# Loading the attention inputs and up-weights first, and moving a weight product behind the first feed-forward tiles

## The chip, the cores and the metric

The kernel runs on one core of a Trainium2 chip. The metric is the device time of one execution in microseconds. The profile adds the span of the core (about 2 us shorter than the time) and the start and duration of every instruction. PE is the matmul engine (TensorE), DVE is VectorE, ACT is ScalarE, POOL is GpSimd, SP is the engine that issues the loads.

## The reference, cut to what matters

```python
# attention: a retention recurrence per batch and head, 4 x 8 x 768 x 64
state = gamma * state + k_t (outer) v_t
y_t   = scale * q_t @ state
# feed-forward on x = y as 3072 x 512
h   = (x @ w1) * (x @ w2) @ w3      # w1, w2: 512 x 1024, w3: 1024 x 1024
out = h @ w_out                      # w_out: 1024 x 512
```

`w3` and `w_out` act one after the other with nothing in between, so the kernel multiplies them once (`W3O = w3 @ w_out`, 64 matmuls of 512 columns and 64 transposes) and uses `W3O` afterwards. The question is *when* that product is made.

## The kernel before

The sequence is cut into 24 chunks of 128 tokens. A chunk needs casts of q, k and v, transposes of q and k, `scores`, the state update `kv`, and `outputs`, which yields x. The feed-forward works on tiles of tokens (0 to 256, 256 to 384, 384 to 512, then 256 each): `a_unit` (w1), `b_unit` (w2, multiplied with the a-half on DVE into `HT`), `o_unit` (`HT` with `W3O`, written out).

```python
# loads, all issued by SP in this order
for i in range(4):
    w3c_st.append(load_w3_columns(i)); wo_st.append(load_wo(i))
w3_st = {f: load_rows(moe_w3, f) for f in range(4, 8)}
load_pair(0)                                   # q, k, v of chunks 0 and 1
w1_st = [load_rows(moe_w1, d) for d in range(4)]
load_pair(1, "qk")
w2_st = [load_rows(moe_w2, 0)]
load_pair(1, "v")
w2_st += [load_rows(moe_w2, d) for d in range(1, 4)]
for n in range(4, 8): load_chunk(n)
# ... constants, cut ...
cast_w3(("c", 0), w3c_st[0])
busy(8)                                        # 8 dummy products on zeros
w3_transpose_columns(0); cast_wo(0)
# ... cut ...
busy(5)
w3_mm_columns(0, acc, lambda: w3_transpose_columns(1))
# ... the rest of the w3 product; from w3_mm(6) on, chunks 0 and 1 are woven in ...
w3_mm(7, chunk1_scores)
# ... tile 0 by weight rows (by_rows), as w1 and w2 land, woven with chunks 2 and 3; cut ...
for i in range(4):
    nc.vector.tensor_tensor(f0.HT[:, 2*i:2*i+2, :], pa[i], ps[i], MULT)
outputs(3, "psA1"); f1.a_unit(6, "psA0"); casts(4)
Tst[0] = kv(3, "psK")
f0.o_unit(0); f0.o_unit(1)
# then steps 4 to 23: each step is one chunk, with up- and output units of
# earlier tiles pulled in between as filler
```

## Time and profile before

| | kernel before |
|---|---|
| time, median of 2 runs | 196.32 us (194.66 to 197.99) |
| time in the later calls, medians of 7 | 195.29, 195.29, 194.92 us |
| span of the profiled run | 193.0 us |
| busy: PE, DVE, ACT, POOL | 96%, 61%, 52%, 44% |

The timeline of PE gives start, duration, engine, line, operation, output and inputs, count, and in brackets the idle time before with what ended it. The durations of matmuls are latencies and overlap, so the pace is read from the distance between starts. These are the first products of the kernel before:

```profile
1.53 3.59 PE L639 MATMUL psZ<-vp 128*128 128x512 f16 x8 [1.53 <-DVE vp L153]
...
6.12 1.24 PE L639 MATMUL psZ<-vp 128*128 128x512 f16 x5
```

Eight dummies of 512 columns need 3.6 us, the next five 1.2 us: the array runs at half its pace at first.

### The profile page before, as it was taken

How to read it: one execution, taken by the hardware profiler on the slowest of the kernel's cores; microseconds unless marked ns; L12 is line 12 of the kernel's file. 1: busy time of each engine (PE TensorE's matmuls, PEld its weight loads, DVE VectorE, ACT ScalarE, POOL GpSimd, SP SyncE). 2: the span in 40 equal slices, each digit the busy share in tenths (PEclk: the TensorE clock that was granted, in tenths of full speed). 3: DMA queues.
4: the chain of work that ended last, by engine and by line, in shares of the span. 5: the costliest groups of instructions: out<-in, count | busy, mean ns of one | idle time of the engine just before them, and what ended most of it. 6: DMA issues, size and time to landing. Idle time of an engine off the chain costs nothing.

```text
span 193.0 us, 4697 instructions
## 1 busy us (share of the span) xinstructions
PE 184.5 (96%) x1777; PEld 139.6 (72%) x1777; DVE 117.4 (61%) x220; ACT 99.5 (52%) x192; POOL 85.6 (44%) x146
## 2 busy tenths in 40 slices
PE   6789999789999999999999999999999999999993
PEld 2335667577797798777977797778777877887752
DVE  3227597699587758656665676565656665753220
ACT  6578555772454464454635463555355545533322
POOL 7600378638872658467152742863326432200000
PEclk9999999999999999999999999999999999999999
DMA  5999999999799999999999999979989930111104
GB/s 207 367 392 389 301 399 323 363 295 209 175 209 229 234 206 242 142 268 215 218 268 213 199 206 232 194 154 277 188 182 196 207 94 20 58 54 54 39 28 155
DMA packets 85030, 40.54 MB, mean 210 GB/s; under 512 B 61328, under 2 KB 80016, under 8 KB 85008
## 3 DMA queue, kind: packets, MB, share of 16 engines
q1 hardware_dynamic: 85008, 40.25, 88.9%
q8 instruction: 14, 0.23, 0.6%
q14 instruction: 8, 0.07, 0.1%
HBM read 29.36 MB, written 6.29 MB: 185 GB/s over the span
## 4 chain that ended last, share of the span: by engine, by line
PE 70%; DMA 17%; POOL 4%; DVE 3%; SPq 2%; issue 1%; ACT 1%; POOLq 0%; DVEq 0%; ACTq 0%
PE psF L508 36%; PE psO L534 18%; DMA stg<-in_v_dram 5%; DMA stg<-in_moe_w_dram 5%; PE psA L437 4%; DMA v<-in_v_dram 4%; DMA kT<-k 3%; SPq L62 2%; PE psY L477 2%; PE psY L478 2%; POOL vp L318 2%; PE psY L480 2%; PE psK L460 2%; PE psF L724 1%; DVE am L442 1%
## 5 line engine op out<-in xcount | busy, mean ns | idle before, releaser
L508 PE MATMUL psF<-xt,w 128*128 128x256 f16 (+1 forms) x736 | 85.0, 266 | 0.0
L508 PEld LDWEIGHTS <-w 128*128 128x128 f16 x768 | 68.2, 98 | 7.2
L524 DVE TENSOR_TENSOR ht<-pa,psF 128x256 f16<-128x256 f32 x88 | 36.5, 416 | 22.5 <-PE psF L508 12.9
L518 ACT COPY pa<-psF 128x256 f32<-128x256 f32 x84 | 31.2, 372 | 34.0 <-PE psF L508 33.5
L442 DVE TENSOR_TENSOR am<-psA,keep 128x512 f16<-128x512 f32 x48 | 31.0, 685 | 21.3 <-PE psA L437 21.2
L534 PE MATMUL psO<-w3o,ht 128*128 128x512 f16 x184 | 43.3, 379 | 0.0
L469 POOL TENSOR_TENSOR t<-s,GS 128x512 f16<-128x512 f32 x15 | 19.3, 1285 | 34.7 <-DVE s L468 34.7
L539 ACT ACTIVATE osb<-psO 128x512 f32<-128x512 f32 x23 | 13.7, 597 | 35.2 <-PE psO L534 35.2
L534 PEld LDWEIGHTS <-ht 128*128 128x128 f16 x184 | 17.8, 98 | 16.9 <-DVE ht L773 0.2
L344 POOL TENSOR_TENSOR vp<-v,VS 128x256 f16<-128x256 f32 x40 | 23.8, 615 | 8.9 <-DMA v<-in_v_dram 4.4
L327 POOL CAST q<-q 128x1024 f16<-128x1024 f32 x12 | 12.6, 1054 | 27.8 <-DMA q<-in_q_dram 27.8
L485 DVE TENSOR_TENSOR xt<-psY,YS 128x512 f16<-128x512 f32 x24 | 17.8, 743 | 4.0 <-PE psY L480 3.6
L477 PE MATMUL psY<-am,vp 128*128 128x128 f16 x96 | 16.8, 219 | 0.6 <-ACT kp L230 0.4
L478 PE MATMUL psY<-am,vp 128*128 128x128 f16 x96 | 16.7, 219 | 0.6 <-DVE vp L318 0.6
L437 PEld LDWEIGHTS <-kp 128*128 128x128 f16 x192 | 12.4, 98 | 5.2 <-DVE kp L228 0.4
L340 POOL CAST k<-k 128x512 f16<-128x512 f32 x20 | 12.2, 611 | 5.0 <-PE psK L460 3.6
L468 DVE TENSOR_TENSOR s<-psK,t 128x512 f32<-128x512 f32 x16 | 11.0, 688 | 3.0 <-PE psK L460 2.5
L411 ACT COPY kp<-kT 64x512 f16<-64x512 f16 x17 | 10.5, 618 | 2.5 <-DMA kT<-k 2.1
L251 DVE COPY w3t<-psW 128x1024 f16<-128x1024 f16 x8 | 5.5, 690 | 10.3 <-PE psW L259 7.9
L437 PE MATMUL psA<-qTd,kp 128*128 128x128 f16 x144 | 11.3, 219 | 0.1
L480 PE MATMUL psY<-qTd,t 128*128 128x128 f16 x60 | 10.8, 219 | 0.0
L412 ACT COPY kp<-kT 64x512 f16<-64x512 f16 x17 | 10.5, 615 | 0.4
(82 smaller groups left out, 190.4 us busy)
## 6 DMA issues: line engine op xcount, KB each, us to landing
stg<-in_moe_w_dram SPq DMA_DIRECT2D x16, 512.0 KB, 7.7
q<-in_q_dram SPq DMA_DIRECT2D x12, 512.0 KB, 5.6
out_dram<-osb SPq DMA_DIRECT2D x23, 256.0 KB, 3.1
k<-in_k_dram SPq DMA_DIRECT2D x20, 256.0 KB, 5.2
v<-in_v_dram SPq DMA_DIRECT2D x20, 256.0 KB, 5.5
stg<-in_moe_w_out_dram SPq DMA_DIRECT2D x4, 512.0 KB, 7.6
stg<-in_k_dram SPq DMA_DIRECT2D x2, 512.0 KB, 10.7
stg<-in_v_dram SPq DMA_DIRECT2D x2, 512.0 KB, 8.2
```

Source lines behind the costliest of these rows:

```text
L344: nc.gpsimd.tensor_tensor(vp[:, :, r, r * 64 : r * 64 + 64], v32[:, :].rearrange("j (p s e) -> j p s e", s=2, e=64)[:, :, r, :], VS[:, :]. ...
L437: nc.tensor.matmul(ps[:, i, r, :], lhsT=kp[:, p, r, :], rhs=queries(n, p), start=True, stop=True)
L442: nc.vector.tensor_tensor(am[:, half * 2 : half * 2 + 2, :, :].rearrange("j p s i -> j (p s) i"), ps[:, :, :, :].rearrange("j p s i -> j ( ...
L469: eng.tensor_tensor(t16[:, :, :], s32[:, :, :], GS[:, :, :], MULT)
L477: nc.tensor.matmul(ps[:, p, :], lhsT=vp[:, p, 0, :], rhs=am[:, p, 0, :], start=True, stop=False)
L478: nc.tensor.matmul(ps[:, p, :], lhsT=vp[:, p, 1, :], rhs=am[:, p, 1, :], start=False, stop=(c == 0))
L480: nc.tensor.matmul(ps[:, p, :], lhsT=Tst[0][:, p, :], rhs=queries(n, p), start=False, stop=True)
L485: nc.vector.tensor_tensor(XT[n // 2][:, :, n % 2 * C : (n % 2 + 1) * C].rearrange("p a (i t) -> p a t i", t=2), ps[:, :, :].rearrange(orde ...
L508: nc.tensor.matmul(ps[:, i * w : (i + 1) * w], lhsT=W[d][:, (f + i) * 128 : (f + i + 1) * 128], rhs=XT[self.tok0 // TB][:, d, c0 : c0 + w] ...
L518: nc.scalar.copy(self.pa[f][:, :], ps[:, :])
L524: nc.vector.tensor_tensor(self.HT[:, f : f + TB // self.width, :].rearrange("p f n -> p (f n)"), self.pa.pop(f)[:, :], ps[:, :], MULT,)
L534: nc.tensor.matmul(psO[:, :], lhsT=self.HT[:, f, tb * 128 : (tb + 1) * 128], rhs=W3O[f][:, :], start=(f == 0), stop=(f == 7),)
```

## The change

The intent is to start the attention some 15 us earlier, since it is a long serial recurrence, and to make `W3O` only when it is first needed. The diff, cut to its core:

```diff
-    w3c_st, wo_st = [], []
-    for i in range(4):
-        w3c_st.append(load_w3_columns(i))
-        wo_st.append(load_wo(i))
-    w3_st = {f: load_rows(moe_w3, f) for f in range(4, 8)}
     load_pair(0)
     w1_st = [load_rows(moe_w1, d) for d in range(4)]
     ...
-    for n in range(4, 8):
-        load_chunk(n)
     # constants: reordered; GS on DVE, keep and VP[2] later on POOL
-    cast_w3(("c", 0), w3c_st[0])
     busy(8)
-    ... busy(5), the whole w3 product ...
     q_cast(0)
+    q_transposes(0)
+    gs_constants()
+    ys_constants()
     pair_casts(0, False, "k")
     ... chunks 0 and 1, then w1's casts ...
     # in tile 0, after the a-half: the loads of w3, w_out and chunks 4 to 7
+    w3c_st, wo_st = [], []
+    ...
     f1.a_unit(6, "psA0")
+    Tst[0] = kv(3, "psK")
+    cast_w3(("c", 0), w3c_st[0])
+    cast_wo(0)
+    for f in (0, 2, 4, 6):
+        f1.b_unit(f)
+    for f in (0, 2, 4, 6):
+        f2.a_unit(f)
+        f2.b_unit(f)
+    w3_transpose_columns(0)
+    ... the whole w3 product ...
+    f0.o_unit(0, lambda: transposes(4))
+    q_transposes(2)
+    f0.o_unit(1)
+    fill.units += f1.o_units() + f2.o_units()     # all the filler of steps 4 and 5
```

More of the change, by code (lines that the diff above doesn't have):

```diff
@@ L153, in zero, with memset_cells @@
         nc.vector.memset(t[:, :, :, :].rearrange("p a b c -> p (a b c)").bitcast(FP), 0.0)
+    def memset_cells(eng, t, value, h):
+        r = (h % 2) * 64
+        eng.memset(t[r : r + 64, h // 2 : h // 2 + 1], value)
     zero(VP[0])
+    ip_i = const.tile([128, H], mybir.dt.int32, name="ip_i")
+    if_i = const.tile([128, 128], mybir.dt.int32, name="if_i")
+    ip2_i = const.tile([128, 2, H], mybir.dt.int32, name="ip2_i")
     ident16 = const.tile([128, 128], HP, name="ident16")
     make_identity(nc, ident16[:, :])
-    ip_i = const.tile([128, H], mybir.dt.int32, name="ip_i")
+    for c in range(2):
+        nc.gpsimd.iota(
+            ip2_i[c * 64 : c * 64 + 64, :, :], pattern=[[1, 2], [0, H]], base=1, channel_multiplier=2
+        )
+    nc.gpsimd.iota(if_i[:, :], pattern=[[1, 2], [2, 64]], base=1, channel_multiplier=0)
     nc.gpsimd.iota(ip_i[:, :], pattern=[[0, H]], base=1, channel_multiplier=1)
-    if_i = const.tile([128, 128], mybir.dt.int32, name="if_i")
-    nc.gpsimd.iota(if_i[:, :], pattern=[[1, 2], [2, 64]], base=1, channel_multiplier=0)
     LGH = const.tile([128, H], FP, name="LGH")
@@ L166 @@
     for h in range(H):
-        r = (h % 2) * 64
-        nc.gpsimd.memset(LGH[:, h : h + 1], -math.log(gam[h]))
-        nc.gpsimd.memset(LGP[r : r + 64, h // 2 : h // 2 + 1], math.log(gam[h]))
-    keep = const.tile([128, 128], FP, name="keep")
-    nc.gpsimd.memset(keep[:, :], 1.0)
-    nc.gpsimd.affine_select(
-        out=keep[:, :], in_=keep[:, :], compare_op=mybir.AluOpType.is_ge, fill=0.0,
-        base=0, pattern=[[1, 2], [2, 64]], channel_multiplier=-1,
-    )
+        nc.vector.memset(LGH[:, h : h + 1], -math.log(gam[h]))
     VS = const.tile([128, H], FP, name="VS")
+    VS2 = const.tile([128, 2, H], FP, name="VS2")
     YS = const.tile([128, NP, 128], FP, name="YS")
@@ L182 @@
     vs_x = const.tile([128, H], FP, name="vs_x")
+    vs2_x = const.tile([128, 2, H], FP, name="vs2_x")
+    nc.vector.tensor_tensor(
+        vs2_x[:, :, :], ip2_i[:, :, :], LGH[:, :].unsqueeze(1).broadcast_to((128, 2, H)), MULT
+    )
     nc.vector.tensor_tensor(vs_x[:, :], ip_i[:, :], LGH[:, :], MULT)
+    for h in range(H):
+        memset_cells(nc.vector, LGP, math.log(gam[h]), h)
     if_f = const.tile([128, 128], FP, name="if_f")
     nc.vector.tensor_copy(if_f[:, :], if_i[:, :])
+    nc.scalar.activation(VS2[:, :, :], vs2_x[:, :, :], AF.Exp)
     nc.scalar.activation(VS[:, :], vs_x[:, :], AF.Exp)
-    for p in range(NP):
-        nc.scalar.activation(YS[:, p, :], if_f[:, :], AF.Exp, scale=LGP[:, p : p + 1])
+    zero(KP[0])
+    zero(KP[1])
+    keep = const.tile([128, 128], FP, name="keep")
     keep2 = const.tile([128, 128], FP, name="keep2")
@@ L197, with last_constants, gs_constants, ys_constants @@
         )
-    ip2_i = const.tile([128, 2, H], mybir.dt.int32, name="ip2_i")
-    for c in range(2):
-        nc.gpsimd.iota(
-            ip2_i[c * 64 : c * 64 + 64, :, :], pattern=[[1, 2], [0, H]], base=1, channel_multiplier=2
-        )
-    zero(KP[0])
-    zero(KP[1])
-    for i in (1, 2):
-        nc.gpsimd.memset(VP[i][:, :, :, :].rearrange("p a b c -> p (a b c)").bitcast(FP), 0.0)
-    nc.gpsimd.memset(GS[:, :, :], 0.0)
-    for h in range(H):
-        p, r = h // 2, (h % 2) * 64
-        nc.gpsimd.memset(GS[r : r + 64, p, r : r + 64], gam[h] ** C)
+    nc.gpsimd.memset(VP[1][:, :, :, :].rearrange("p a b c -> p (a b c)").bitcast(FP), 0.0)
+    def last_constants():
+        nc.gpsimd.memset(keep[:, :], 1.0)
+        nc.gpsimd.affine_select(
+            out=keep[:, :], in_=keep[:, :], compare_op=mybir.AluOpType.is_ge, fill=0.0,
+            base=0, pattern=[[1, 2], [2, 64]], channel_multiplier=-1,
+        )
+        nc.gpsimd.memset(VP[2][:, :, :, :].rearrange("p a b c -> p (a b c)").bitcast(FP), 0.0)
+    def gs_constants():
+        nc.vector.memset(GS[:, :, :], 0.0)
+        for h in range(H):
+            p, r = h // 2, (h % 2) * 64
+            nc.vector.memset(GS[r : r + 64, p, r : r + 64], gam[h] ** C)
+    def ys_constants():
+        for p in range(NP):
+            nc.scalar.activation(YS[:, p, :], if_f[:, :], AF.Exp, scale=LGP[:, p : p + 1])
     XT = {}
@@ L617, in step @@
         fill.pull(share * 0.25, ready)
-        if n == 5:
-            fill.units.pop(0)
-            ffn[1].o_unit(0, lambda: [outputs(n), transposes(6)])
-        else:
-            outputs(n)
+        outputs(n)
         Tst[0] = t_new
-        if n not in (4, 5):
+        if n != 4:
             transposes(n + 1)
@@ L643, in cast_wo @@
         cast_to(WO[i][:, :, :].rearrange("p a n -> p (a n)"), wo_st[i][:, :], i == 0)
-    cast_w3(("c", 0), w3c_st[0])
     busy(8)
-    acc = [ps_f.tile([128, DM], FP, tag="psF", name="psW")[:, :] for _ in range(3)]
-    acc.append(ps_at.tile([128, DM], FP, tag="psY", name="psWy")[:, :])
-    w3_transpose_columns(0)
-    cast_wo(0)
-    VS2 = const.tile([128, 2, H], FP, name="VS2")
-    vs2_x = const.tile([128, 2, H], FP, name="vs2_x")
-    nc.vector.tensor_tensor(
-        vs2_x[:, :, :], ip2_i[:, :, :], LGH[:, :].unsqueeze(1).broadcast_to((128, 2, H)), MULT
-    )
@@ L656 @@
-    nc.scalar.activation(VS2[:, :, :], vs2_x[:, :, :], AF.Exp)
-    busy(5)
-    cast_w3(("c", 1), w3c_st[1])
-    w3_mm_columns(0, acc, lambda: w3_transpose_columns(1))
-    cast_wo(1)
-    cast_w3(("c", 2), w3c_st[2])
-    w3_mm_columns(1, acc, lambda: w3_transpose_columns(2))
-    cast_wo(2)
-    cast_w3(("c", 3), w3c_st[3])
-    w3_mm_columns(2, acc, lambda: w3_transpose_columns(3))
-    cast_wo(3)
-    cast_w3(4, w3_st[4])
-    cast_w3(5, w3_st[5])
-    w3_mm_columns(3, acc)
-    w3_transpose(4)
@@ L671 @@
-    w3_transpose(5)
-    cast_w3(6, w3_st[6])
-    cast_w3(7, w3_st[7])
     q_cast(0)
+    q_transposes(0)
+    gs_constants()
+    ys_constants()
     pair_casts(0, False, "k")
+    pair_casts(0, True, "k")
     pair_casts(1, False, "k")
+    pair_casts(1, True, "k", nc.scalar)
+    last_constants()
+    transposes(0)
+    transposes(1, "psK")
     pair_casts(0, False, "v")
+    pair_casts(0, True, "v")
     pair_casts(1, False, "v")
-    pair_casts(1, True, "v", nc.gpsimd)
-    w3_mm(4, lambda: w3_transpose(6))
@@ L681 @@
-    w3_mm(5, lambda: w3_transpose(7))
-    pair_casts(0, True, "k")
-    pair_casts(1, True, "k")
-    q_transposes(0)
-    pair_casts(0, True, "v")
-    for r in (0, 1):
-        nc.gpsimd.tensor_copy(W1[r][:, :], w1_st[r][:, :])
-    w3_mm(6, lambda: transposes(0), 3)
-    transposes(1, "psK")
-    scores(0)
-    cast_w(W1, w1_st, 2, False)
-    def chunk1_scores():
-        first.append(kv(0, "psT"))
-        scores(1)
-        outputs(0)
-    first = []
-    w3_mm(7, chunk1_scores)
-    Tst[0] = first[0]
+    scores(0)
@@ L701 @@
+    first = kv(0, "psT")
+    scores(1)
+    outputs(0)
+    Tst[0] = first
+    pair_casts(1, True, "v")
+    cast_w(W1, w1_st, 0, False)
     outputs(1, "psT")
     Tst[0] = kv(1, "psK", nc.vector)
+    cast_w(W1, w1_st, 1, False)
+    cast_w(W1, w1_st, 2, False)
     cast_w(W1, w1_st, 3, False)
@@ L754 @@
     transposes_back(3)
+    w3c_st, wo_st = [], []
+    for i in range(4):
+        w3c_st.append(load_w3_columns(i))
+        wo_st.append(load_wo(i))
+    w3_st = {f: load_rows(moe_w3, f) for f in range(4, 8)}
+    for n in range(4, 8):
+        load_chunk(n)
     cast_w(W2, w2_st, 1, False)
@@ L775 @@
     f1.a_unit(6, "psA0")
-    casts(4)
-    Tst[0] = kv(3, "psK")
-    f0.o_unit(0)
+    Tst[0] = kv(3, "psK")
[3 more added lines that the diff above has]
+        f1.b_unit(f)
+    f2 = ffn[2]
+    for f in (0, 2, 4, 6):
+        f2.a_unit(f)
+        f2.b_unit(f)
+    w3_transpose_columns(0)
+    acc = [ps_f.tile([128, DM], FP, tag="psF", name="psW")[:, :] for _ in range(3)]
+    acc.append(ps_at.tile([128, DM], FP, tag="psY", name="psWy")[:, :])
+    cast_w3(("c", 1), w3c_st[1])
+    w3_mm_columns(0, acc, lambda: w3_transpose_columns(1))
+    cast_wo(1)
+    cast_w3(("c", 2), w3c_st[2])
+    w3_mm_columns(1, acc, lambda: w3_transpose_columns(2))
+    cast_wo(2)
+    cast_w3(("c", 3), w3c_st[3])
+    w3_mm_columns(2, acc, lambda: w3_transpose_columns(3))
+    cast_wo(3)
+    cast_w3(4, w3_st[4])
+    cast_w3(5, w3_st[5])
+    w3_mm_columns(3, acc)
+    w3_transpose(4)
+    w3_transpose(5)
+    cast_w3(6, w3_st[6])
+    cast_w3(7, w3_st[7])
+    w3_mm(4, lambda: w3_transpose(6))
+    casts(4)
+    w3_mm(5, lambda: w3_transpose(7))
+    w3_mm(6)
+    w3_mm(7)
+    casts(5)
+    f0.o_unit(0, lambda: transposes(4))
+    q_transposes(2)
     f0.o_unit(1)
-    for t in range(1, NT):
-        late = ffn[t - 1].o_units() if t > 1 else []
+    fill.units += f1.o_units() + f2.o_units()
+    for t in range(3, NT):
+        late = ffn[t - 1].o_units() if t > 3 else []
         units = ffn[t].ab_units()
-        if t == 1:
-            units = units[1::2]
         for i in range(0, len(units), 8):
@@ L791 @@
     fill.units.append((0, 1.73, lambda: ffn[NT - 1].last_o_unit(ffn[NT - 1].width // 128 - 1)))
-    fill.run(2)
-    casts(5)
-    transposes(4)
-    q_transposes(2)
-    fill.run(4)
     for n in range(4, NSTEP):
```

## The prediction

> **What bounds the kernel now.** I read the slices of the page first, then the groups, then the chain of waits, then the timelines of TensorE (PE) and VectorE (DVE) up to 62 us. Slices of the page (40 slices of 4.83 us, busy tenths):
> ```profile
> PE   6789999789999999999999999999999999999993
> DMA  5999999999799999999999999979989930111104
> GB/s 207 367 392 389 301 399 323 363 295 209 175 209 229 234 206 242 142 268 215 218 268 213 199 206 232 194 154 277 188 182 196 207 94 20 58 54 54 39 28 155
> ```
> From slice 9 on PE is full; only the front, about 50 us, has room, and there the loads also run at their peak rate. So the change can only alter PE's idle time in the front.
>
> How much is there? The chain of waits gives PE's pace where it is dense: 32 up-product matmuls in 3.49 us (109 ns each), 8 output matmuls of 512 columns in 1.73 us, 8 of 128 columns in 0.45 us. With the counts of the code: up-products 768 x 0.109 = 83.7 us; outputs 24 x 1.73 = 41.5; scores 24 x 0.445 = 10.7; attention outputs 272 x 0.0556 = 15.1; kv 80 x 0.0556 = 4.4; transposes of q and k 52 x 0.0556 = 2.9; w3 with w_out 64 x 0.0556 + 64 x 0.2165 = 17.4. Sum **175.8 us** of needed PE work in a span of 193.0: 17.2 us are idle (or filled with dummy products on zeros). The last output matmul is done at about 190.1, so 2.9 us are tail. At 46.35, after kv of chunk 3, the needed work done is scores 1.8, attention outputs 2.45, kv 0.9, transposes 1.8, tile 0 7.0, the a-half of tile 1 1.75, w3 17.4, together 33.1: so **13.3 us** of idle lie before 46.35 and only 1.0 us after it.
>
> The front of the timeline of VectorE is the part that decides the case (start, duration, what):
> ```profile
> 36.29 0.43 DVE L228 COPY kp<-psT 64x512 f16<-64x512 f16 x1 [1.05 <-ACT kp L426]
> 36.75 0.69 DVE L228 COPY stg<-psF 128x512 f32<-128x512 f32 x1
> ...
> 42.38 0.68 DVE L468 TENSOR_TENSOR s<-psK,t 128x512 f32<-128x512 f32 x1
> 43.09 1.83 DVE L318 TENSOR_TENSOR vp<-stg,VS 64x256 f16<-64x256 f32 x2
> 44.95 1.88 DVE L773 TENSOR_TENSOR ht<-stg,psF 128x512 f16<-128x512 f32 x3
> 46.75 0.68 DVE L773 TENSOR_TENSOR ht<-stg,psG 128x512 f16<-128x512 f32 x1
> 47.35 0.73 DVE L485 TENSOR_TENSOR xt<-psY,YS 128x512 f16<-128x512 f32 x1
> 47.97 0.68 DVE L468 TENSOR_TENSOR s<-psK,t 128x512 f32<-128x512 f32 x1
> ```
> From the copy of chunk 2's keys at 36.29 to the state sum of chunk 3 at 48.65, DVE has hardly a gap (busy 12.20 of 12.68 us in that stretch): 12.4 us of serial DVE work for chunks 2 and 3 and tile 0. PE hides its end, because output tile 0 needs nothing of it:
> ```profile
> 46.35 3.62 PE L534 MATMUL psO<-w3o,ht 128*128 128x512 f16 x16
> 49.80 1.06 PE L508 MATMUL psF<-xt,w 128*128 128x128 f16 x16
> ```
> And the early PE idle is partly filled with w3 work that needs only weights.
>
> **What the Trainium skill says.** "TensorE: Matmul & The Clock Gate", Part 1: the array starts at half clock, takes about 3.4 us of sustained work to be released, and falls back after an idle window; 512 columns then cost 426.7 instead of 215.7 ns. The trace agrees: the first 8 dummy products fill 3.59 us (about 0.43 us apart), the next 5 take 1.24 us. "DMA: Bandwidth & Descriptors", Specifications: runs of 512 B or more reach line rate. Here they do not quite: the weight rows land 1.34 us apart (casts that wait for them at 10.54, 11.85, 13.32, 14.61, 15.96, 17.25), the q, k, v pairs in 512 B runs 1.7 to 2.0 us apart. "SBUF — State Buffer", Who interferes with whom: a DVE operation with two SBUF inputs and a GpSimd operation that reads SBUF exclude each other. The v scaling on DVE took 1.83 us beside the state product on GpSimd (POOL) at 43.20, 1.17 us elsewhere; it agrees, and it will recur.
>
> **The change part by part.**
> (1) Loads. The 14 transfers of q, k, v, w1, w2 that stood behind 12 of w3 and w_out come first. In the trace they take 21.7 us together (w3's last cast starts at 19.8, w2's last at 41.5), and the first transfer lands near 5. Estimates: q0 at 5.5, k0 7.2, v0 9, last row of w1 14.5, q1 16, k1 17.7, v1 21, last row of w2 **24.8**; w3 from 26 to 42. The chunks from 4 on follow at the same time as now.
> (2) Chunks 0 and 1. With nothing else on PE: k casts to 8.3, transposes, two ScalarE (ACT) copies to 10.2, scores. DVE then has am 1.28, t 0.68, am 1.28, xt 0.74, v scaling 1.17, and after the outputs of chunk 1 xt 0.74: from about 10.6 to 17.4. Behind that, in PE's order: second half of w1's row 0 0.45, rows 1 and 2 1.75, q transposes 0.45, three blocks of row 3 0.33, transposes of chunk 2; so DVE's key copy begins at about 21.0, against 36.29 now: **15.3 us earlier**. Half clock costs perhaps 1.2 us of it, since PE is mostly idle from 5 to 17.
> (3) Chunks 2 and 3 and tile 0. The same 12.4 us of DVE work follow in the same order. w2 comes 16.7 us earlier (41.5 to 24.8), more than the 14 to 15 by which the key copy moves, so DVE is the limit, not the load. kv of chunk 3 ends at 46.35 - 15.3 + 1.2 = **32.3**, with 33.1 - 17.4 = 15.7 us of work done: 16.6 us of idle, against 13.3. So taking w3 out of the front loses 3.3 us: it is 17.4 us of filler removed for 14.1 us gained.
> (4) After kv of chunk 3 the b-half of tile 1 now follows at once. PE gets three PSUM banks done (1.33 us), then needs a bank that DVE frees: DVE has 2.3 us left of its chain, then the new w_out cast 0.72, then the first product 0.42. Wait: 2.3 + 0.7 + 0.4 + 0.1 - 1.3 = **2.2 us**; before, 3.46 us of outputs hid this.
> (5) w3 begins with 8 transposes whose copy (0.69 plus latency) nothing covers, since the dummies are gone: **1.0 us**, and 0.3 us in the gaps seen before at 18.2 and 18.8. Its loads are in time and its 17.4 us run dense.
> (6) Steps 4 and 5 have only two output tiles as filler, and ACT must evict the second (0.6) before it copies chunk 6's keys (1.24): scores of chunk 6 wait about **1.3 us**.
> Sum: 3.3 + 2.2 + 1.3 + 1.3 = 8.1 us. Span 193.0 + 8.1 = 201.1. The profiled run was 195.03 us at a span of 193.0, so add 2.0: **203 us**.
>
> **The rivals.** *It gains*: w3 work fills the time in which PE now waits, and attention starts 15 us earlier. Speaks for it: the 10 us of idle or dummies before 15 us. Against it: until w2 has landed at 24.8 and been cast, only 13 us of PE work exist, so some 12 to 13 us of idle stay even with perfect chains; the best case is a span near 191, time 193. *It cancels*: the half clock does not bite, DVE's 12.4 us pack tighter as v and w2 come earlier, and the waits of (4) and (6) are shorter: +2 to +4 us, time 197 to 199. *The loads bind*: w3's seventh transfer needs the buffer of chunk 3's v, free only at about 30 when DVE has scaled it; if the queue runs dry there, w3 and then chunks 4 to 7 come later, and scores of chunk 6 wait for its transposed keys more than I took: time 205 to 208. The DMA row is full but the loads for step n are issued four steps ahead, so I give it little. After step 8 the order is as before and dense.
>
> **Range and chances.** The front (3) is uncertain by 2 us, waits (4) to (6) by 1.5 us together, the run by 1 us: 198.5 to 207. Against 196.3, a gain of over 2% would need a span near 190, below even the best case: 0.04. Within 2% needs 4 of the 8 us to vanish: 0.20. Slower by over 2%: 0.76.
>
> **What would show it.** (1) holds if the last w2 cast starts at 24 to 26; (2) if DVE's key copy of chunk 2 starts at 20 to 23; (3) if DVE is full from there for 12 us and kv of chunk 3 ends at 31 to 34; (4) to (6) if PE waits for DVE at tile 1's fourth b-unit, for the first w3 copy, and at the scores of chunk 6. PE's slices should show the idle before 32 us and be full after about 40. I am wrong if kv of chunk 3 ends before 29, or if PE idles in the dense part because the loads of chunks 4 to 8 slip.

## The result, and the profile after

| | before | changed |
|---|---|---|
| time, median of 2 | 196.32 us | 206.16 us (205.46 to 206.86) |
| ratio, 95% interval | 1 | 1.0557 (1.0433 to 1.068) |
| the same in a second call | 1 | 1.0506 (1.0476 to 1.0535) |
| span of the profiled run | 193.0 us | 205.1 us |
| end of kv of chunk 3 on PE | 46.35 us | 35.33 us |
| last output product starts | 188.17 us | 200.22 us |

A ratio is the mean time of one kernel's runs over that of the other's runs of the same rounds, so it is not quite the ratio of the medians quoted. The two medians alone would give 1.050.

The change makes the kernel 5 to 5.6% slower. The direction was predicted; the size was put too low, at 203 us and 3.4%. The time lies near the upper end of the range (198.5 to 207 us), while the two marks of the front lie outside theirs, as the last part shows. The slices of the page after:

```profile
PE   7286989689999989999999999999999999999994
GB/s 155 341 359 336 390 379 383 372 228 243 101 3 51 142 264 194 248 166 273 226 160 250 242 222 184 233 196 174 214 201 221 201 117 77 51 54 0 51 54 153
PEclk9999999999999999999999999999999999999999
```

PE now has holes up to slice 9 (slices of 5.13 us) and a small one at slice 15. The loads move at 330 to 390 GB/s early on, as before, and then pause (3 GB/s in slice 12): no wait of PE in this profile ends with a load, and the experiments test whether the loads matter indirectly. The chain of VectorE that answers to the one shown of before:

```profile
25.70 0.43 DVE L234 COPY kp<-psT 64x512 f16<-64x512 f16 x1 [0.46 <-ACT kp L432]
...
32.08 1.83 DVE L324 TENSOR_TENSOR vp<-stg,VS 64x256 f16<-64x256 f32 x2
33.94 1.88 DVE L750 TENSOR_TENSOR ht<-stg,psF 128x512 f16<-128x512 f32 x3
35.74 0.68 DVE L750 TENSOR_TENSOR ht<-stg,psG 128x512 f16<-128x512 f32 x1
36.34 0.72 DVE L491 TENSOR_TENSOR xt<-psY,YS 128x512 f16<-128x512 f32 x1
36.96 0.68 DVE L474 TENSOR_TENSOR s<-psK,t 128x512 f32<-128x512 f32 x1
37.55 0.68 DVE L234 CAST wo<-stg 128x1024 f16<-128x1024 f32 x1
```

It is the same unbroken chain, 11.9 us long (12.4 before), but it starts 10.6 us earlier (25.70 against 36.29) and not the 14 to 15 us that were predicted. On PE, the front and what follows the chain:

```profile
6.26 1.03 PE L372 MATMUL psTq<-ident,q 128*128 128x128 f16 x8 [1.15 <-POOL q L333]
10.38 1.01 PE L427 MATMUL psT<-ident,k 128*128 128x128 f16 x8 [3.08 <-DVE k L319]
...
20.84 1.49 PE L693 MATMUL psF<-xt,w 128*128 128x256 f16 x6
22.11 0.63 PE L693 MATMUL psG<-xt,w 128*128 128x256 f16 x2
...
35.33 1.50 PE L514 MATMUL psF<-xt,w 128*128 128x128 f16 x24
38.62 4.18 PE L514 MATMUL psF<-xt,w 128*128 128x128 f16 x72 [1.78 <-DVE ht L530]
42.63 0.61 PE L265 MATMUL psW<-ident,w3h 128*128 128x128 f16 x8
44.03 1.04 PE L286 MATMUL psW<-wo,w3t 128*128 128x512 f16 x4 [0.79 <-DVE w3t L257]
...
72.82 0.23 PE L443 MATMUL psA<-qTd,kp 128*128 128x128 f16 x1 [0.57 <-ACT kp L417]
73.46 0.56 PE L443 MATMUL psA<-qTd,kp 128*128 128x128 f16 x7 [0.41 <-ACT kp L418]
```

Six w1 products of 256 columns take 1.27 us from start to start (20.84 to 22.11), 0.21 us each, where the dense part has 0.109: half pace, at 20 us into the kernel. The keys' transposes at 10.38 waited 3.08 us for a cast of k on DVE. Later, the waits at 38.62, 44.03 and 72.82 are the ones that the prediction named.

Where the 12.1 us of span went: up to the end of kv of chunk 3, PE has 35.33 us for 15.7 us of work, 19.6 us idle or slow, against 13.3 before: **6.3 us**. From there to the start of the last output product there are 164.9 us against 141.8, and 17.4 of the difference are the w3 product that has moved there: **5.7 us** of new waits. Together 12.0.

### The profile page after: what moved, and what is told of

Its sections match the earlier page's. It is cut to its first block, busy times and chain, and to the rows that moved or that the text cites. A ratio compares the mean times of both kernels' runs of the same rounds, so it can differ in the third digit from the quotient of the medians.

```text
span 205.1 us, 4684 instructions
## 1 busy us (share of the span) xinstructions
PE 188.4 (92%) x1772; PEld 143.8 (70%) x1772; DVE 118.8 (58%) x246; ACT 101.1 (49%) x195; POOL 79.4 (39%) x117
## 4 chain that ended last, share of the span: by engine, by line
PE 82%; DVE 7%; DMA 5%; issue 2%; ACT 2%; POOL 1%; DVEq 0%; ACTq 0%; POOLq 0%
PE psF L514 35%; PE psO L540 19%; PE psA L443 5%; PE psW L299 3%; PE psF L693 3%; PE psY L483 2%; PE psY L484 2%; DMA kT<-k 2%; PE psW L286 2%; DMA q<-in_q_dram 2%; PE psK L466 2%; PE psY L486 2%; DVE am L448 2%; DVE vp L324 1%; PE psTq L372 1%
## 5 line engine op out<-in xcount | busy, mean ns | idle before, releaser
L530 DVE TENSOR_TENSOR ht<-pa,psF 128x256 f16<-128x256 f32 x88 | 36.6, 417 | 23.3 <-PE psF L514 12.1
L475 POOL TENSOR_TENSOR t<-s,GS 128x512 f16<-128x512 f32 x15 | 19.6, 1308 | 60.1 <-DVE s L474 60.1
L483 PE MATMUL psY<-am,vp 128*128 128x128 f16 x96 | 17.6, 226 | 2.2 <-DVE vp L324 1.6
L443 PEld LDWEIGHTS <-kp 128*128 128x128 f16 x192 | 13.2, 101 | 7.0 <-ACT kp L417 0.7
L484 PE MATMUL psY<-am,vp 128*128 128x128 f16 x96 | 17.6, 226 | 0.2 <-DVE vp L324 0.2
L483 PEld LDWEIGHTS <-vp 128*128 128x128 f16 x96 | 9.7, 102 | 2.9 <-POOL q L333 1.8
```

Of the source, the lines that this page charges most:

```text
L443: nc.tensor.matmul(ps[:, i, r, :], lhsT=kp[:, p, r, :], rhs=queries(n, p), start=True, stop=True)
L475: eng.tensor_tensor(t16[:, :, :], s32[:, :, :], GS[:, :, :], MULT)
L483: nc.tensor.matmul(ps[:, p, :], lhsT=vp[:, p, 0, :], rhs=am[:, p, 0, :], start=True, stop=False)
L484: nc.tensor.matmul(ps[:, p, :], lhsT=vp[:, p, 1, :], rhs=am[:, p, 1, :], start=False, stop=(c == 0))
L530: nc.vector.tensor_tensor(self.HT[:, f : f + TB // self.width, :].rearrange("p f n -> p (f n)"), self.pa.pop(f)[:, :], ps[:, :], MULT,)
```

## The experiments

Theory A: the front is set by a serial chain through DVE, ACT and PE. Two things stretch it beyond what was predicted: constants that DVE writes ahead of the key cast, and the half pace of PE. Behind the chain, the filler is missing that used to hide DVE's work. Rival B: the loads of w1, q, k, v and w2 set the front, so shortening the chain gives nothing. Rival C, for the later part: the loads of w3 or of chunks 4 to 8 would be waited for instead.

All edits are to the changed kernel except where stated. Each table entry is from runs beside the kernel before; kv(3) is the end of kv of chunk 3 on PE. Span, key copy and kv(3) are those of the one profiled run, which need not be the median one: it is the slowest of four in the control and the fastest of four in e5.

| run | time, median (range of 4) | ratio to before | span | key copy of chunk 2 | kv(3) |
|---|---|---|---|---|---|
| changed, control | 205.24 (204.47 to 205.90) | 1.0506 | 204.0 | 24.56 | 34.20 |
| e1_gs | 204.03 (202.63 to 205.00) | 1.0433 | 203.1 | 23.72 | 33.35 |
| e2_warm | 204.92 (204.75 to 205.08) | 1.0482 | 203.0 | 23.10 | 32.73 |
| e3_gs_warm | 202.73 (202.73 to 202.88) | 1.0374 | 200.8 | 21.03 | 31.41 |
| e4_poolv | 204.03 (203.92 to 205.07) | 1.045 | 202.1 | 24.45 | 33.15 |
| e5_cover | 204.89 (204.30 to 205.89) | 1.0495 | 202.4 | 24.49 | 34.13 |
| e8_steps | 203.02 (202.36 to 204.95) | 1.041 | 201.9 | 24.62 | 34.25 |
| e9_all | 200.88 (200.55 to 201.03) | 1.0298 | 199.2 | 21.08 | 31.40 |
| e10_all_steps | 198.86 (198.73 to 199.05) | 1.0199 | 196.9 | 20.96 | 31.18 |

### Control: the changed kernel again (after0)

> The changed kernel itself, as a control beside the other three. The half-clock theory expects its runs to spread by 1 to 2 us (the moment at which the array is released differs from run to run), more than those of the kernels with dummy products (0.2 to 0.3 us in the first call), and a median near 205.5.

The median was 205.24 and the four runs spread by 1.4 us. In its profile the key copy starts at 24.56 instead of 25.70, because the array is at full pace at other moments than in the first profile:

```profile
PEclk9858899999999999999999999999999999999999
6.21 0.62 PE L372 MATMUL psTq<-ident,q 128*128 128x128 f16 x8 [1.11 <-POOL q L333]
...
18.12 0.39 PE L466 MATMUL psK<-vp,k 128*128 128x128 f16 x4
18.34 0.60 PE L693 MATMUL psF<-xt,w 128*128 128x128 f16 x6
...
21.20 0.64 PE L693 MATMUL psG<-xt,w 128*128 128x256 f16 x2
21.63 1.02 PE L693 MATMUL psF<-xt,w 128*128 128x256 f16 x6
```

Four products of 128 columns take 0.22 us at 18.12, so the array is at full pace there (it is from 15.15 us on); the two of 256 columns at 21.20 take 0.43, half pace again. The switches lie at about 15.15, 18.6 and 22.0 us, 3.4 us apart, which agrees with the free-running window that the Trainium skill describes ("TensorE: Matmul & The Clock Gate", Part 1). The first line of the fence is the clock row of this page: after the first slice it follows these switches (5 in the slice from 10.2 to 15.3 us), where the row of the first profile reads 9 throughout. In both pages it reads 9 in the first slice, where the dummies ran at half pace: it reads full until the trace records a first change. The eight dummies are the same in both runs, yet q's transposes behind them ran at full pace here (0.62 us) and at half pace in the first profile (1.03 us). In the first profile the same part stayed at half pace until about 23.4. So the changed kernel has no single time: its front depends on when the array is released, and that differs from run to run; that the phase of the window decides it is argued, as no run sets the phase. Over all runs, the four other kernels that keep the sparse front spread by 1.2 to 2.6 us, and the four with dummy products by 0.2 to 0.5 us. (The kernel before spread by 0.6, 0.8 and 1.9 us, so not every spread has this cause.) In 10 of the 22 runs with the sparse front the mean granted clock is below 0.99 (0.964 to 0.989); in every other run listed it is 0.998 or more. A difference of less than 1 us between kernels of the first kind is therefore read from waits in the trace and not from the times.

### e1_gs: the constants off the key cast's way

```diff
     q_cast(0)
-    q_transposes(0)
     gs_constants()
+    q_transposes(0)
     ys_constants()
```

> The nine memsets of GS on VectorE (8.14 to 9.95 us in the changed kernel) are issued before the copies of q's transposes, where VectorE idles 3.0 us. Theory A (a serial chain through VectorE sets the front): the key cast comes 1.7 us earlier, kv of chunk 3 ends near 33.6 instead of 35.3 us, and the time falls by 1.5 to 1.8 us (0.8%). Rival B (the arrival of w1, w2, q1, k1, v1 sets the front): the later chain stays where it is, kv of chunk 3 at 35.3 us, time unchanged within 0.3 us.

The VectorE timeline of the changed kernel, and then of this one, at the key cast:

```profile
8.14 0.48 DVE L212 MEMSET GS<- 128x512 f32 x1
8.70 1.25 DVE L215 MEMSET GS<- 64x64 f32 x8
9.88 0.36 DVE L319 CAST k<-stg 64x512 f16<-64x512 f32 x1
```
```profile
4.90 1.25 DVE L215 MEMSET GS<- 64x64 f32 x8
...
7.64 0.81 DVE L319 CAST k<-stg 64x512 f16<-64x512 f32 x1
```

The memsets fit into a hole that DVE has before q's transposes. The keys' transposes start at 8.60 instead of 10.38, 1.8 us earlier, and w1's first products at 17.28 instead of 19.13, 1.85 us earlier. kv of chunk 3 ends at 33.35, 2.0 us ahead of the first profile but only 0.85 ahead of the control, whose array was at full pace for part of that stretch (outputs of chunk 1), where this one was at half pace until about 21.3 us. The ratio falls from 1.0506 to 1.0433, but these are different calls and the intervals (1.0476 to 1.0535, 1.0367 to 1.0498) overlap: the shift in the trace is the evidence. There theory A holds; rival B, which expected no shift at all, fails.

### e2_warm: dummy products in PE's waits

```diff
-    busy(8)
+    warm(12)          # products on a zero tile of its own
     q_cast(0)
     q_transposes(0)
     ...
+    warm(14)          # before chunk 0's keys
     ...
+    warm(3)           # before scores(0);  warm(2) before scores(1)
+    warm(2)           # before outputs(0); warm(6) after it
```

> Dummy products on zeros (39 of 512 columns in place of 8) fill PE's waits up to chunk 1. Theory A, half clock: the first w1 rows run at 0.65 us for 6 matmuls of 256 columns instead of 1.27, VectorE's copy of chunk 2's keys starts at 22.5 to 23.5 instead of 25.7 us, time lower by 2.5 to 3 us (1.3%). Rival B (loads set the front): matmuls are shorter but kv of chunk 3 stays at 35.3 us and the time too.

PE of this kernel at the w1 products that took 1.27 us:

```profile
19.49 0.82 PE L705 MATMUL psF<-xt,w 128*128 128x256 f16 x6
20.14 0.38 PE L705 MATMUL psG<-xt,w 128*128 128x256 f16 x2
```

They take 0.65 us. The key copy starts at 23.10: 2.6 us sooner than in the first profile of the changed kernel, 1.5 us sooner than in the control. The gain in span is 2.1 and 1.0 us. So the mechanism is there, but against the control the expected 2.5 to 3 us were not reached: that run had had full pace for part of the stretch itself, and about half a microsecond is given back by a wait of 0.41 us for keys at 88.8 us that the control does not have. The time, 204.92 us, is only just below the control's 205.24; what the dummies plainly remove is the spread (0.3 us).

### e3_gs_warm: both

The two edits together, with `warm(6)` in place of `warm(14)`.

> Both: GS early and dummy products. Theory A: the two add, chunk 2's key copy at 21 to 22 us (where the prediction put it without the half clock), kv of chunk 3 at 31 us, time lower by 4 to 4.7 us (2.1%), to about 201. Rival B: no more than 0.5 us. A mixed result, with the first wait moving to the arrival of q1 or k1 (about 17 us), would give 2.5 to 4 us.

The key copy:

```profile
21.03 0.43 DVE L236 COPY kp<-psT 64x512 f16<-64x512 f16 x1 [0.46 <-ACT kp L434]
```

The prediction had put it at "about 21.0" without the half clock. It takes both edits to get there, 4.7 us sooner than in the first profile: 1.8 from the constants (e1) and the remaining 2.9, by subtraction, from the pace. The span falls by 4.3 us to 200.8, the ratio to 1.0374. kv(3) ends 3.9 us sooner and not 4.7: between the key copy and kv(3), two waits have grown, 0.69 us for a v scaling on POOL and 0.58 (0.16 before) for one on DVE. So the gain is mixed, as the expectation allowed, but the wait moved to v of chunk 2 and not to q1 or k1: v's load landed at 22.01 us, and its two scalings then ran side by side on GpSimd (from 22.08) and VectorE (22.81 to 24.30, 1.49 us instead of 0.75).

### e4_poolv: work taken off VectorE

```diff
-    scores(2, between=lambda: pair_casts(2, True, "v"))
+    pair_casts(2, True, "v", nc.gpsimd)
+    pair_casts(3, True, "v", nc.gpsimd)
+    scores(2)
     ...
-    pair_casts(3, True, "v")
```

> The two moved-half v scalings of chunks 2 and 3 go from VectorE (0.75 and 1.83 us) to GpSimd, which is idle from 23.3 to 32.2 us in the changed kernel. Theory A (from chunk 2's key copy on, VectorE is the limit): VectorE's chain is 2.6 us shorter, the wait of 1.78 us at tile 1's fourth b-unit nearly goes, time lower by 1.5 to 2.6 us. Rival B (w2's arrival sets this stretch): kv of chunk 3 stays within 0.3 us of 35.3 and the time is unchanged.

```profile
33.15 1.50 PE L514 MATMUL psF<-xt,w 128*128 128x128 f16 x24
35.66 4.18 PE L514 MATMUL psF<-xt,w 128*128 128x128 f16 x72 [1.00 <-DVE ht L530]
```

From the key copy to the end of kv of chunk 3, PE needs 8.70 us instead of 9.64 in the control, and the wait at tile 1's fourth b-unit is 1.00 us instead of 1.77. That is 1.7 us, and the span falls by 1.9. The wait did not "nearly go", because PE itself got faster by 0.9 us and DVE then waited 1.1 us for PE's w2 products. VectorE is the limit of this stretch, the loads are not: rival B expected kv(3) to stay, and it ended 1.05 us earlier while the last w2 row landed at 25.55 us against 25.65.

### e5_cover: work under the waits behind the chain

```diff
     cast_w3(("c", 0), w3c_st[0])
-    cast_wo(0)
     for f in (0, 2, 4, 6): f1.b_unit(f)
     for f in (0, 2, 4, 6):
         f2.a_unit(f)
+        if f == 0: cast_wo(0)
+        if f == 6: w3_transpose_columns(0)
         f2.b_unit(f)
-    w3_transpose_columns(0)
```

> The w_out cast of VectorE moves behind tile 1's b-units, and w3's first transposes move ahead of tile 2's last b-unit. Theory A (these waits are on the path that sets the end, since PE is dense behind them): the wait of 1.78 us at tile 1's fourth b-unit falls to about 1.1 and the wait of 0.79 us for the first w3 copy goes; time lower by 1.3 to 1.6 us than the changed kernel's. Rival C (the loads of w3 or of the chunks from 4 on would be waited for instead): the gain is given back before the scores of chunk 6, time unchanged.

The waits fell as expected, from 1.77 to 1.17 us and from 0.79 to 0.34, 1.05 us in all, and PE finished the outputs of chunk 5 at 69.8 instead of 70.9 us. No new wait took their place; three of the four waits at steps 6 and 7 are the same and the fourth (0.42 us) is gone, so rival C finds no support. From kv(3) to the start of the last output product, which leaves the front out, e5 takes 163.4 us and the control 164.9. The time does not show it: 204.89 against 205.24 us with ranges that overlap. By the times alone the trial is inconclusive; e9 below repeats it on a front that does not scatter.

### e8_steps: the filler of steps 4 and 5

```diff
-    for f in (0, 2, 4, 6):
-        f2.a_unit(f)
-        f2.b_unit(f)
-    fill.units += f1.o_units() + f2.o_units()
-    for t in range(3, NT):
+    for t in range(2, NT):      # tile 2's up-products are filler again
```

> Tile 2's up-products go back from before the w3 product into the filler of steps 4 and 5, as in the kernel before. Theory A: the waits at steps 6 and 7 (0.57 and 0.41 us at the scores of chunk 6, 0.41 and 0.39 us for the eviction of a-halves) go, since filler is longer than the chain of casts, transposed loads and copies; VectorE's waits before the product stay as they are, or grow by up to 0.5 us at the first w3 copy; time lower by 1.0 to 1.8 us. Rival C (the late loads of chunks 6 to 8 bind): the wait at the scores of chunk 6 stays.

All four waits at steps 6 and 7 are gone. PE now runs into the scores of chunk 6 without a pause:

```profile
67.82 1.89 PE L540 MATMUL psO<-w3o,ht 128*128 128x512 f16 x8
69.55 0.61 PE L443 MATMUL psA<-qTd,kp 128*128 128x128 f16 x8
```

The front is that of the control (kv(3) at 34.25 against 34.20) and the waits before the product are unchanged (1.78 and 0.79). The span is 2.1 us shorter, and so is the stretch from kv(3) to the last output product (162.8 against 164.9 us); the ratio is 1.041. The expectation of 1.0 to 1.8 us was slightly low. Rival C fails here: the transposed keys of chunk 6 are there when PE has other work for long enough.

### e7_before_nodummy: the kernel before without its dummies

```diff
-    busy(8)
 ...
-    busy(5)
```

> The kernel before without its 13 dummy products. Theory A: the w3 product itself is dense enough to release the clock[...], and this stretch waits for loads anyway, so the time rises by 0 to 1.5 us, far less than the 5 us of half clock that the changed kernel has. Rival (the dummies, not the w3 product, keep the front fast): over 3 us slower.

195.76 us (195.49 to 196.47), ratio 1.0029 (1.0003 to 1.0056), against a median of 195.29 for the kernel before in the same call. PE of this run:

```profile
10.60 1.06 PE L280 MATMUL psW<-wo,w3t 128*128 128x512 f16 x2
11.45 1.06 PE L280 MATMUL psWy<-wo,w3t 128*128 128x512 f16 x2
...
14.47 0.59 PE L280 MATMUL psW<-wo,w3t 128*128 128x512 f16 x2
14.90 0.59 PE L280 MATMUL psWy<-wo,w3t 128*128 128x512 f16 x2
```

Without dummies PE stays at half pace until about 14 us (0.43 us for each product of 512 columns, then 0.22), yet the kernel loses only 0.3%. In the kernel before, the pace of this stretch is given by loads, and PE has time to spare; in the changed kernel, the half pace sits on the chain. The same state of the array costs 0.5 us in one order of work (1.0 us between the two profiled spans, 194.0 and 193.0) and about 1.7 to 2.9 in the other, as the last part works out; the expectation's 5 us were too many.

### e9_all and e10_all_steps: everything together

e9 takes e3, e5 and the chunk-3 half of e4; e10 adds e8, casts the first w_out rows on ACT, leaves that cast where the changed kernel has it, and puts w3's first transposes before tile 1's last b-unit.

> Everything that the single trials named, in the new order of loads: GS early, dummy products, chunk 3's moved v half scaled on GpSimd, the w_out cast and w3's first transposes under tile 1 and 2. Theory A: from the 200.8 us span of the GS and dummies trial another 1.5 us (wait at tile 1's fourth b-unit) and 0.5 to 1 us (first w3 copy) less, a span of 198.3 to 199, a time of 200.5, ratio 1.027 to before. Rival: the waits are on the path only one at a time, and the loads of v of chunk 2 and w2 now bind, span not below 200.

> The same, with tile 2's up-products back in steps 4 and 5 and the first w_out cast on ScalarE. Theory A: another 1.5 to 2 us less, a span of 196.5 to 197.5, ratio 1.015 to 1.02: close to the kernel before but not below it, since PE has 12 to 13 us without work until w2 has landed, where the kernel before has w3's product to do. If the new order of loads were as good as the old and only these waits made it slow, it would reach 193 or less.

e9 has a span of 199.2 us and a ratio of 1.0298: 1.6 us less than e3, as the waits say (0.40 and 0.34 us in place of 1.78 and 0.79). e10 has 196.9 us and 1.0199, another 2.3 us. The single gains add up roughly, and the kernel is still 2.0% slower than before. Where its remaining 3.9 us lie: PE has 31.18 us for 15.7 us of work up to kv(3), 15.5 idle against 13.3 before (2.2 us), and 1.6 to 1.7 us lie behind it, of which waits of 0.66 and 0.39 us stand at the first w3 products and in its middle. In e10 the loads come close to binding. PE waits for the two scalings of v of chunk 2, whose load landed at 21.80 us, and ScalarE's w2 casts wait for loads:

```profile
23.44 0.22 PE L485 MATMUL psY<-am,vp 128*128 128x128 f16 x1 [0.55 <-POOL vp L326]
24.24 0.22 PE L486 MATMUL psY<-am,vp 128*128 128x128 f16 x1 [0.59 <-DVE vp L326]
...
24.39 1.04 ACT L238 CAST w<-stg 128x1024 f16<-128x1024 f32 x1 [0.24 <-DMA stg<-in_moe_w_dram]
25.70 1.04 ACT L238 CAST w<-stg 128x1024 f16<-128x1024 f32 x1 [0.26 <-DMA stg<-in_moe_w_dram]
```

In the changed kernel the three casts run back to back and wait for nothing but ScalarE:

```profile
27.73 2.94 ACT L236 CAST w<-stg 128x1024 f16<-128x1024 f32 x3
```

So the last w2 row lands near 25.7 us (24.8 was predicted). PE does not wait for it in e10 either: its cast ends at 26.74 and its products start at 28.52, with no wait of PE between 24.9 and 31.2 us. Until w2 lands this order of loads has, by the prediction's count, only some 13 us of work for PE; the old order has the 17.4 us of the w3 product to give it. That this shortage of work, and not the serial chain of chunks 0 to 3 itself, holds the rest of the gap is argued and not shown. No version tried here beats the kernel before.

## Why the prediction was right or wrong

**Right: the direction and its reason.** Taking the w3 product out of the front removes 17.4 us of filler and brings attention forward by less than that. e10 shows it most plainly: with the named waits removed or shortened, kv of chunk 3 ends 15.2 us earlier than before, and the new order is still 2.0% behind.

**Right: step (1).** By the landing records of the trace, the last row of w1 landed at 13.85 us (14.5 predicted), k1 at 17.41 (17.7), the last row of w2 at 25.70 (24.8).

**Wrong: the size of the front, step (2).** The prediction put the key copy at 21.0, allowed 1.2 us for the half clock, and so had kv of chunk 3 end at 32.3. It ended at 35.33 in the first profile and at 34.20 in the control. Two terms were mis-sized:

- "Half clock costs perhaps 1.2 us of it": about **2.9 us** in the first profile (4.7 us of e3, less the 1.8 of e1), and by the same subtraction about 1.7 in the control. I counted it as a small share of a sparse stretch, but from 17.24 us on everything that PE did up to the release at about 23.4 was on the path. The size is itself uncertain by more than 1 us from run to run.
- "k casts to 8.3": the DVE half of that cast ended at 10.2, because the diff puts `gs_constants()` between `q_transposes` and the key casts, and DVE works in order. **1.8 us** (e1). The instruction order of DVE showed this before any run; I read the order and did not add up what stood ahead of the key cast.

1.7 of the first and 1.8 of the second are 3.5 us at the key copy; the stretch from the key copy to kv(3) was 0.4 shorter than taken, which leaves the 3.0 us by which kv(3) was late. (The prediction took 1.17 us for a v scaling on DVE; in both places where it read that, GpSimd was scaling v as well. Beside an idle GpSimd, at 27.48 us in the changed kernel, it took 0.75: that is the 0.4.) In the control kv(3) was late by 1.9 us, inside the 2 us of uncertainty that the prediction gave the front. The rest of the miss, 12.1 against 8.1 us in span, is about 0.9 in the later part.

**Right: step (3).** VectorE is the limit from the key copy on (11.9 us, predicted 12.4), and e4 shows that the loads are not. One reading is slightly off: the 12.20 busy of 12.68 us belong to the window from 35.97 us, not from the copy at 36.29.

**Nearly right: steps (4) to (6).** Predicted 2.2, 1.3 and 1.3 us. Measured waits: 1.78; 0.79 and 0.39; 0.57 and 0.41. Two waits of 0.41 and 0.39 us for a-half evictions at steps 6 and 7 were not foreseen; e8 removes all four. The 0.39 is also missing in e3 and e5, which leave these steps alone, so its cause is not settled. Each wait also costs about 0.16 us of latency, which the 5.7 us contain.

**The signs that were named.** The last w2 cast began near 29.6 and not at 24 to 26: not a late load, but ScalarE that was late itself. The key copy (25.70) and kv(3) (35.33) fell outside their windows, which pointed at step (2) at once. The measured time fell into the range of the rival in which the loads bind (205 to 208 us), but not for its reason: e8 removes the waits at chunk 6 without touching a load.

**Open.** When the array is last released in the sparse front was observed (about 21 to 23.4 us; in two of six profiles also for one window after the dummies) but not controlled; the 3.4 us steps of the control fit a free-running window, but no run sets its phase. The times of e5 do not settle its gain; the 1.5 us behind kv(3) rest on one profile of each kernel.

## What to carry to other kernels

Work that needs only early loads is filler for a front that is bound by loads and latency; moving it later is worth only what the work that takes its place can fill. Add up the in-order queue of each helper engine ahead of the first critical cast, constants included. A sparse front can run the array at half pace, and the page's clock row may show it (the control) or not (the first profile): read the distance between starts of equal matmuls as well. A few dummies may not help: eight were not enough in four of six profiles here, twelve, with more dummies in the later waits, were in four of four.

## What the Trainium skill lacked or had wrong

- "TensorE: Matmul & The Clock Gate", Part 1: about 3.4 us of sustained activity release the array, and an idle window puts it back. These runs show it less simple. The eight dense dummies (3.6 us) were followed by full pace in the kernel before and, at q's transposes, in the control and e1 (0.62 us for eight), but by half pace in the first profile, e4, e5 and e8 (1.03 to 1.04 us). And the control fell back at 18.6 us although PE had been busy for 1.55 of the last 3.4 us. What the page lacks is a figure for work that follows a sparse stretch: here full pace came 3.5 us (e8) to 5.8 us (the first profile) and 5.9 us (e7) after the products had become almost unbroken, up to nearly two windows. I budgeted 1.2 us of loss where 2.9 were paid.
- The same page warns that traced clock events are unreliable. Here those in the packed traces agree with the spacing of products: one release at 23.40 us in the first profile; switches at 15.20, 18.61 and 22.02 in the control. What misleads is the profile page's clock row, which reads 9 until the first change that was recorded: in the first profile also while products of 128 columns stood 0.107 us apart (from 19.13 us).
- "DMA: Bandwidth & Descriptors", Specifications: runs of 512 B reach line rate. In the kernel before, transfers of 0.5 MB of q, k and v in 512 B runs landed 1.71 to 1.84 us after the transfer before them (one 2.38), those of weight rows in runs of 4 KB 1.27 to 1.39.
